# A state space and MLP layer on one core: one block transposed by TensorE, the rest rows of w1 loaded twice, LayerNorm written in one part, and a new order

## The chip, the cores and the metric

The kernel runs on one core of one Trainium2 chip. The core has five engines that run side by side, each with its own list of instructions: TensorE (PE; PEld is its loading of weights), VectorE (DVE), ScalarE (ACT), GpSimd (POOL) and SyncE (SP). SyncE here only issues DMAs, and ScalarE issues a few as well. Engines wait for one another by semaphores. Data are computed on in SBUF, TensorE writes its products into banks of PSUM, and DMAs move data between the chip's memory and SBUF, some of them transposing on the way. The metric is the device time of one execution in microseconds (us); the lower the better.

## The reference

The input x has 2048 tokens of 448 channels. `xn` is its LayerNorm. Two branches read it: a diagonal state space model with 448 complex states, and an MLP with a second LayerNorm, 1792 hidden units, gelu, and silu at its end.

```python
xn = layernorm(x)
# state space branch
dt = exp(log_dt); Lam_bar = exp(dt * Lam)
B_bar = ((Lam_bar - 1) / Lam)[:, None] * B          # B, C complex, 448 x 448
h[t] = Lam_bar * h[t-1] + B_bar @ xn[t]             # 2048 steps
s = 2 * real(C @ h) + xn * Dskip
# MLP branch
g = silu(gelu(layernorm(xn) @ w1 + b1) @ w2 + b2)   # w1 448 x 1792, w2 1792 x 448
out = x + s * g
```

## The kernel before

**Tiles and groups.** The 2048 tokens are worked on in four groups of 512. A group has two blocks of 256 tokens, and a block has two parities: a partition holds two neighbouring tokens, the even one (parity 0) and the odd one (parity 1), so that each tile is 128 tokens of 448 channels. LayerNorm writes two versions of a group: `xn` for the state space branch (buffer `xn_sb`) and `xm` for the MLP, LayerNorm applied twice (buffer `xn2_sb`). The profile's names of buffers don't always tell the two apart on the side of the reader: some rows say `xn_sb` for either. Both are transposed, because TensorE contracts over partitions; the results are `xnT` and `xn2T`.

**The first product, w1.** A channel count of 448 is three blocks of 128 rows and one of 64. All matmuls of `one_mm` (L666) contract over 64 rows, the upper and the lower half of the partitions side by side, so the last 64 rows of w1 are needed on both halves. In the kernel before, chunks of columns of w1 are loaded by SyncE (`ldw1`, L339): chunk 0 of two column blocks of 128, and three of four. One load brings w1's last 64 rows to the upper half of slot 3, and after each chunk a copy by ScalarE or VectorE puts the needed rows on the lower half. For this the LayerNorm rows are laid out as 512 columns that overlap: columns 0 to 383, and then 320 to 447, written as two parts (L410, L451, L452). Products go through gelu on ScalarE (L673) into `gT`.

**Group 0's opening.** `first_stats` (L384) and `first_apply` (L403) make `xm` of group 0 directly. Block 0 is transposed by TensorE, eight transposes against an identity into PSUM (L415), and copied out by VectorE and ScalarE. Block 1 is transposed by a DMA that SyncE issues (L77). `mm1_run` then makes the first product with matmuls 256 wide, block 0 and block 1 mixed. `dummies` (L382) are matmuls of a constant that keep TensorE going before its data are there.

**The rest.** The second product (w2) is L792 and L795 with full rows and the last 64; in the last group L853 makes it with tokens on the partitions. The bias columns of the end, Dskip and b2, are turned by small matmuls (`skip_columns`, L563 and L564) and copied from PSUM into `db`. B_bar is made from the parameters (`parameters`, `tables`, `lb`: L601, L602), and three transposing DMAs make `BT` from `Bn`. The input projection `bu` (L698) multiplies `xnT` by `BT`; VectorE scans (L757); L816, L817, L821 and L822 multiply with C, in the last group L866 and L869. `ln_scale` (L424) makes the factors of LayerNorm out of the statistics, either on VectorE by an inverse root of its own (L431, L432, L436 to L441) or on GpSimd by a power (L431 to L435). A sine for the parameters' complex exponentials is a polynomial on GpSimd (L500 to L506).

**What sets the order.** Nothing is scheduled at run time. Each piece of work is recorded as a task with the names that it reads and writes (`Plan.add`); from these the program works out the semaphore waits. The list `ORDER` says in which order the tasks are given out to the engines' lists, and `SECOND` says which tasks that were recorded with two engines (`either`, L65) take the second one. A DMA is a task of the engine that issues it, and stands in that engine's list: an instruction of SyncE that waits holds up all later DMAs of its queue.

Of the kernel before, what the change touches and what calls it, by code (L numbers as in the profile page):

```python
# [979 lines left out]
```

## Time and profile before

| | |
|---|---|
| median of 3 runs | 144.18 us (144.06 to 144.89) |
| profiled execution | 145.18 us |
| its span | 143.4 us |
| granted TensorE clock | 1.0 |
| PE busy | 137.7 us, 96% of the span |
| DVE busy | 126.0 us, 88% |
| ACT busy | 105.9 us, 74% |
| POOL busy | 24.7 us, 17% |

The profile is of one execution, which took 145.18 us; its span, from the first to the last instruction recorded, is 143.4 us, and all times inside the profile count from the start of that span. A row of a timeline gives the start of a run of equal instructions, how long the run took, the engine, the line of the kernel, the operation with output and inputs, and how many there are; a bracket at the end gives the idle time of the engine just before and what ended it. A matmul's end is modelled, so that two in a row overlap in the rows; where the pace matters, one counts from start to start. A row of grouped instructions has the busy time and the mean of one.

### The profile page before, as it was taken

How to read it: one execution, taken by the hardware profiler on the slowest of the kernel's cores; microseconds unless marked ns; L12 is line 12 of the kernel's file. 1: busy time of each engine (PE TensorE's matmuls, PEld its weight loads, DVE VectorE, ACT ScalarE, POOL GpSimd, SP SyncE). 2: the span in 40 equal slices, each digit the busy share in tenths (PEclk: the TensorE clock that was granted, in tenths of full speed). 3: DMA queues.
4: the chain of work that ended last, by engine and by line, in shares of the span. 5: the costliest groups of instructions: out<-in, count | busy, mean ns of one | idle time of the engine just before them, and what ended most of it. 6: DMA issues, size and time to landing. Idle time of an engine off the chain costs nothing.

```text
span 143.4 us, 3549 instructions
## 1 busy us (share of the span) xinstructions
PE 137.7 (96%) x1422; PEld 90.9 (63%) x1422; DVE 126.0 (88%) x275; ACT 105.9 (74%) x197; POOL 24.7 (17%) x83
## 2 busy tenths in 40 slices
PE   7999998999999989999999999999999999999991
PEld 7879953464455854566558844588777677665560
DVE  2979878998999679999999989993699998999994
ACT  3699959999996879879889359451777999928300
POOL 3389760256000700001000000200000001000000
DMA  4979997799997961010010745099830000003233
GB/s 101 240 238 249 311 331 184 152 245 184 199 189 148 151 134 35 0 32 0 7 32 0 61 108 110 0 199 193 160 126 9 0 5 0 18 5 69 49 119 128
DMA packets 38530, 16.21 MB, mean 113 GB/s; under 512 B 32937, under 2 KB 38066, under 8 KB 38514
## 3 DMA queue, kind: packets, MB, share of 16 engines
q1 hardware_dynamic: 38352, 15.92, 49.5%
q8 instruction: 11, 0.18, 0.5%
q10 hardware_dynamic: 162, 0.07, 0.2%
q14 instruction: 5, 0.04, 0.1%
HBM read 6.09 MB, written 1.84 MB: 55 GB/s over the span
## 4 chain that ended last, share of the span: by engine, by line
PE 63%; DMA 14%; DVE 13%; SPq 4%; ACT 1%; issue 1%; POOL 1%; DVEq 0%; ACTq 0%
PE psum L667 15%; PE psum L698 13%; PE psum L792 9%; PE psum L853 7%; DMA Bn<-in_A_B_re_dram 6%; PE psum L817 5%; DMA xnT<-xn_sb 5%; PE psum L816 5%; PE psum L382 3%; DMA Cr<-in_A_C_im_dram 3%; SPq L78 3%; DVE tmp L601 2%; DVE Bn L602 2%; PE psum L869 2%; PE psum L866 2%; DVE xn_sb L451 2%
## 5 line engine op out<-in xcount | busy, mean ns | idle before, releaser
L667 PE MATMUL psum<-xn2T,w_sb 64*128 64x512 bf16 (+1 forms) x490 | 46.5, 334 | 0.7 <-DMA w_sb<-in_B_w_dram 0.3
L673 ACT ACTIVATE gT<-psum,b1f 128x512 bf16<-128x512 f32 (+1 forms) x70 | 37.5, 607 | 4.5 <-PE psum L667 4.2
L667 PEld LDWEIGHTS psum<-xn2T,w_sb 64*128 64x128 bf16 x490 | 26.6, 108 | 13.9 <-ACT gT L673 1.0
L792 PE MATMUL psum<-gT,w_sb 128*128 128x512 bf16 x126 | 28.0, 379 | 0.7 <-ACT gT L673 0.6
L698 PE MATMUL psum<-xnT,BT 64*128 64x256 bf16 x392 | 25.0, 269 | 0.4 <-DVE u_sb L721 0.4
L698 PEld LDWEIGHTS psum<-xnT,BT 64*128 64x128 bf16 x392 | 19.2, 94 | 6.7 <-issue 1.0
L792 PEld LDWEIGHTS psum<-gT,w_sb 128*128 128x128 bf16 x126 | 11.9, 98 | 15.6 <-issue 1.5
L757 DVE TENSOR_TENSOR_SCAN s_w<-vs,dk 128x1048 f32<-128x1048 bf16 (+1 forms) x8 | 16.3, 2057 | 0.1
L452 ACT ACTIVATE xn_sb<-x_all,lnw 128x448 bf16<-128x448 bf16 (+2 forms) x16 | 10.0, 665 | 5.4 <-DMA xnT<-xn_sb 3.8
L853 PE MATMUL psum<-w_sb,gT 128*128 128x448 bf16 x56 | 10.9, 352 | 0.0
L474 ACT ACT_TABLE_LOAD x8 | 10.3, 1283 | 0.4
L305 ACT ACTIVATE ue<-psum 128x512 bf16<-128x512 f32 (+1 forms) x12 | 6.4, 562 | 5.3 <-PE psum L698 5.2
L451 DVE TENSOR_SCALAR xn_sb<-x_all,lnw 128x448 bf16<-128x448 bf16 (+2 forms) x24 | 8.0, 362 | 0.9 <-DVE lnw L441 0.5
L853 PEld LDWEIGHTS psum<-w_sb,gT 128*128 128x128 bf16 x56 | 5.5, 98 | 4.8 <-ACT psum L305 0.2
L305 ACT ACTIVATE vs<-s_w 64x258 bf16<-64x258 f32 (+2 forms) x11 | 6.5, 612 | 2.7 <-DVE s_w L757 2.6
L816 PE MATMUL psum<-hx,CZ 128*128 128x256 bf16 x63 | 8.4, 275 | 0.0
L817 PE MATMUL psum<-Bn,CQ 128*128 128x256 bf16 x63 | 8.2, 273 | 0.2 <-DVE Bn L777 0.2
L767 POOL TENSOR_TENSOR cur<-ang 128x8 f32<-128x8 f32 x2 | 0.4, 204 | 41.6 <-DVE ang L766 41.6
L798 ACT ACTIVATE g_sb<-psum,db 128x512 bf16<-128x512 f32 (+1 forms) x12 | 7.1, 629 | 0.6 <-PE psum L792 0.6
L369 DVE BATCH_NORM_STATS2 lnst<-x_all 128x6 f32<-128x448 bf16 x12 | 7.1, 613 | 0.4 <-DMA x_all<-in_A_x_dram 0.4
L816 PEld LDWEIGHTS psum<-hx,CZ 128*128 128x128 bf16 x63 | 5.9, 98 | 2.3 <-issue 0.4
L824 DVE TENSOR_TENSOR t<-psum,g_sb 128x512 bf16<-128x512 f32 (+1 forms) x12 | 7.1, 614 | 0.1
(161 smaller groups left out, 207.1 us busy)
## 6 DMA issues: line engine op xcount, KB each, us to landing
x_all<-in_A_x_dram SPq DMA_DIRECT2D x3, 448.0 KB, 4.3
w_sb<-in_B_w_dram SPq DMA_DIRECT2D x3, 448.0 KB, 5.3
out_dram<-Bn SPq DMA_DIRECT2D x6, 224.0 KB, 2.7
w_sb<-in_B_w_dram SPq DMA_DIRECT2D x3, 384.0 KB, 5.5
w_sb<-in_B_w_dram SPq DMA_DIRECT2D x2, 224.0 KB, 4.5
...
```

Source lines behind the costliest of these rows:

```text
L305: kb.either(("act", [lambda e, o=o, i=i: e.activation(o, i, ACT.Copy) for o, i in pairs]), ("dve", [lambda e, o=o, i=i: e.tensor_copy(o, i ...
L451: kb.either(("dve", [lambda e, o=o, i=i: e.tensor_scalar(o, i, rs, nb, op0=ALU.mult, op1=ALU.add) for o, i in parts]), ("act", [lambda e, ...
L452: ("act", [lambda e, o=o, i=i: e.activation(o, i, ACT.Identity, bias=nb, scale=rs) for o, i in parts]),
L474: kb.add("act", lambda e: e.preload_act_table_set(what), reads, writes, sem=name)
L667: return lambda e: e.matmul(dst(bk[k]), w1_sb[rows, d, fcol(2 * j + k)], rhs[rows, d], start=not second and n == 0, stop=second and n == 3)
L673: act(lambda e, k=k, fi=fi: e.activation(gT[:, gb, fi, cols], psum[:, bk[k], cols], ACT.Gelu_apprx_tanh, bias=b1f[:, fi:fi + 1]), ["b1f", ...
L698: fns.append(lambda e, rows=rows, bank=bank, m=m, o=o, n=n: e.matmul(psum[:, bank, c * NK:(c + 1) * NK].rearrange("p (b c) -> p b c", b=2) ...
L757: dve(lambda e, so=so, vi=vi, di=di: e.tensor_tensor_scan(so, vi, di, 0.0, ALU.add, ALU.mult), ["v", "vl", "vz", "dk", "dk01"] + ["v3"] * ...
L792: pe([lambda e, fi=fi: e.matmul(psum[:, bk, :], w2_sb[:, fi, 128 * j:128 * j + 128], gT[:, gb, fi, :], start=fi == 0, stop=fi == NF - 1) f ...
L816: pe([lambda e, k=k: e.matmul(par(psum[:, bk, :], 1), CZ[:, k, cols], halves(hx[:, hb, k, 1:NK + 1]), start=False, stop=k == 6, skip_group ...
L817: pe([lambda e, k=k: e.matmul(par(psum[:, bk, :], 0), CQ[:, k, cols], halves(hz[:, hb, k, :]), start=False, stop=k == 6, skip_group_check= ...
L853: pe([lambda e, fi=fi: e.matmul(P, gT[:, gb, fi, 128 * q:128 * q + 128], w2_sb[:, fi, :], start=False, stop=fi == NF - 1, skip_group_check ...
```

## The change

Five things are changed; all of them end in a new `ORDER` and a new `SECOND`.

1. **Block 1 of group 0.** The transposing DMA of SyncE is gone. `first_apply` now has TensorE transpose block 1 as well: `turn` gives three full transposes and two of 64 columns, one to each half of the partitions, for each parity. Block 0 is done in the same way, so that there are 20 transposes in place of 8, and two more copies out of PSUM, both given to ScalarE. `mm1_run` now starts with more work of block 0 ahead of block 1's.
2. **w1.** Its last 64 rows are loaded twice by ScalarE's queue, to the upper and to the lower half; the copies `w1c_*` are gone. The chunks are three, of 4, 4 and 6 column blocks.
3. **LayerNorm in one part.** `ln_apply` and `first_apply` write 448 columns with one instruction, and a new helper `tail` copies the last 64 of them for the MLP's rows too, so that the transposing DMA finds 512 columns.
4. **Small things.** Dskip's and b2's rows are loaded by SyncE's queue and no longer by ScalarE's; b1 comes in rows of another width, turned by ten small matmuls; one clamp and one negation of the parameters become one instruction and two exponentials; an absolute value may be made by VectorE; four dummies are left out.
5. **Order and engines.** For example, group 1's `ln_scale` was on VectorE and is on GpSimd; group 0's goes the other way. The copy into `db` was ScalarE's and is VectorE's.

Lines move: L667 becomes L660, L698 L691, L792 L785, L795 L788, L415 L375 and L376, L382 L381, L451 L450, L458 L386 (the new helper), L601 and L602 L594 and L595, L305 and L306 L304 and L305.

Three places show the new order. The rows are each engine's instructions as they stand in its list, with the semaphores that they wait for (`s_dve` is VectorE's, `s_d26` that of a DMA).

SyncE's list, before, from the transposition of group 1's `xm` (xn2T) on:

```order
L77 DMA_TRANSPOSE xn2T<-xn_sb 128x16x128 [waits s_dve,s_act]
L78 DMA Bn<-in_A_B_re_dram 64x448
L78 DMA x_all<-in_A_x_dram 128x2x896
L77 DMA_TRANSPOSE xnT<-xn_sb 128x16x128 [waits s_dve]
L77 DMA_TRANSPOSE Cr<-in_A_C_re_dram 128x3x448
L77 DMA_TRANSPOSE Cr<-in_A_C_im_dram 128x3x448
L77 DMA_TRANSPOSE BT<-Bn 128x16x128 [waits s_dve] x2
L77 DMA_TRANSPOSE BT<-Bn 128x24x128 [waits s_dve]
```

The same stretch after the change:

```order
L77 DMA_TRANSPOSE Cr<-in_A_C_re_dram 128x3x448
L77 DMA_TRANSPOSE xn2T<-xn_sb 128x16x128 [waits s_dve]
L77 DMA_TRANSPOSE BT<-Bn 128x16x128
L77 DMA_TRANSPOSE Cr<-in_A_C_im_dram 128x3x448
L77 DMA_TRANSPOSE xnT<-xn_sb 128x16x128 [waits s_dve]
L77 DMA_TRANSPOSE BT<-Bn 128x16x128
L77 DMA_TRANSPOSE BT<-Bn 128x24x128 [waits s_dve]
```

C's first transposition now stands ahead of xn2T's, the first BT right behind it, and group 0's xnT after that; the loads of Bn and x that stood between come ahead of all of these.

TensorE's list, before, around the first matmuls of the input projection (L698), with the second product of group 0 (L792) between:

```order
L698 MATMUL psum<-xnT,BT 128x256 [waits s_d27,s_d26]
L698 MATMUL psum<-xnT,BT 128x256 x11
L792 MATMUL psum<-gT,w_sb 128x512 [waits s_act]
L792 MATMUL psum<-gT,w_sb 128x512 x5
L792 MATMUL psum<-gT,w_sb 128x512 [waits s_act]
L792 MATMUL psum<-gT,w_sb 128x512 x7
L698 MATMUL psum<-xnT,BT 128x256 [waits s_d28]
L698 MATMUL psum<-xnT,BT 128x256 x11
```

And after, where L691 is the input projection and L660 the first product of group 1:

```order
L691 MATMUL psum<-xnT,BT 128x256 [waits s_d25,s_d23,s_d24]
L691 MATMUL psum<-xnT,BT 128x256 x11
L660 MATMUL psum<-xn2T,w_sb 128x512 [waits s_pe]
L660 MATMUL psum<-xn2T,w_sb 128x512 x7
L691 MATMUL psum<-xnT,BT 128x256 [waits s_pe]
L691 MATMUL psum<-xnT,BT 128x256 x15
L660 MATMUL psum<-xn2T,w_sb 128x512 [waits s_act]
L660 MATMUL psum<-xn2T,w_sb 128x512 x5
L691 MATMUL psum<-xnT,BT 128x256 [waits s_act,s_d26]
L691 MATMUL psum<-xnT,BT 128x256 x11
```

The rows that wait for the third BT are those of `s_d28` before and of `s_d26` after. Ahead of them now stand 28 matmuls of the input projection in place of 12, fewer of group 1's first product (90 in place of 98), and none of the 14 of L792, which come later.

VectorE's list, before, where group 1's `xm` is made (L451, ahead of it the last step of `ln_scale`, L441):

```order
L441 SCALAR_TENSOR_TENSOR lnw<-lnmv,lnw 128x8 [waits s_dve]
L451 TENSOR_SCALAR xn_sb<-x_all,lnw 128x384 [waits s_dve,s_d24]
L451 TENSOR_SCALAR xn_sb<-x_all,lnw 128x128
L451 TENSOR_SCALAR xn_sb<-x_all,lnw 128x384
L451 TENSOR_SCALAR xn_sb<-x_all,lnw 128x128
L451 TENSOR_SCALAR xn_sb<-x_all,lnw 128x384 [waits s_dve]
L451 TENSOR_SCALAR xn_sb<-x_all,lnw 128x128
```

And after, from a B_bar step on (L594, L595; L567 are steps of the table `s_w`):

```order
L595 SCALAR_TENSOR_TENSOR Bn<-Bn,cw,tmp 128x512 [waits s_dve]
L567 SCALAR_TENSOR_TENSOR s_w<-dk,cw,s_w 128x258
L305 COPY db<-psum 128x8 [waits s_pe]
L506 TENSOR_TENSOR cw<-cw 128x4
L509 TENSOR_SCALAR cw<-cw 128x4
L595 SCALAR_TENSOR_TENSOR Bn<-Bn,cw,tmp 128x512 [waits s_dve]
L450 TENSOR_SCALAR xn_sb<-x_all,lnw 128x448 [waits s_pool]
L450 TENSOR_SCALAR xn_sb<-x_all,lnw 128x448
L567 SCALAR_TENSOR_TENSOR s_w<-dk,cw,s_w 128x258
L450 TENSOR_SCALAR xn_sb<-x_all,lnw 128x448 [waits s_dve] x2
L567 SCALAR_TENSOR_TENSOR s_w<-dk,cw,s_w 128x258
L386 COPY xn_sb<-xn_sb 128x4x64 [waits s_dve]
```

The copy into `db` is now here, and `xm` waits for GpSimd's `ln_scale` (`s_pool`), is made in four instructions, and has the tail copy behind it.

The diff, with the numbers of `ORDER` and `SECOND` cut to a line each and the comparisons of small indices left out:

```diff
-14 363 16 41 0 9 10 15 1 17 13 2 11 3 22 12 5 18 4 19 21 90 23 26 24 91 93 42 25 89 28 92 94 30 43 95 104 103 45 44 64 109 105 50 46 96 20 110 47 108
+14 0 16 36 9 10 2 11 5 15 17 3 13 1 12 19 18 4 23 24 84 20 25 21 85 37 87 22 83 35 38 86 88 40 8 39 89 27 41 105 44 97 28 42 45 102 7 106 98 43 57 90
...
-29 31 45 51 53 54 60 61 62 63 64 65 78 79 80 82 83 84 111 181 204 205 206 208 210 212 216 218 220 229 234 236 238 242 250 254 256 258 270 274 278 328
+41 44 47 48 49 51 55 56 60 62 64 67 72 76 78 79 82 101 170 171 172 173 177 201 204 206 208 212 214 216 225 228 230 232 234 236 238 242 244 250 273 277
...
-            CH = ((0, 2), (2, 4), (6, 4), (10, 4))
+            CH = ((0, 4), (4, 4), (8, 6))
...
                 ld("sp", w1_sb[:, 0:3, a:a + w], dram_ap(B_w1, a, [[F, 128], [128 * F, 3], [1, w]]), [f"w1_{c}"])
-                copy([(w1_sb[0:64, 3, a:a + w], w1_sb[64:128, 2, a:a + w])], [f"w1_{c}"], [f"w1c_{c}"])
...
+            for h in (1, 0):
+                ld("act", w1_sb[64 * h:64 * h + 64, 3, :], dram_ap(B_w1, 384 * F, [[F, 64], [1, F]]), [f"w1r{h}"])
             ldw1(0)
-            ld("sp", w1_sb[64:128, 3, :], dram_ap(B_w1, 384 * F, [[F, 64], [1, F]]), ["w1r"])
...
-            def tcols(b, par, d):
-                a = par * 512 + (0, 128, 256, 320)[d]
-                return xn2_sb[:, b, a:a + 128]
+            def turn(b, par, bank):
+                row, o = xn2_sb[:, b, par * 512:par * 512 + D], psh[:, bank, 0:512].rearrange("p (d c) -> p d c", d=4)
+                return [lambda e, d=d: e.transpose(o[:, d], row[:, 128 * d:128 * d + 128], ident[:, :]) for d in range(3)] \
+                    + [lambda e, h=h: e.transpose(o[h, 3], row[:, 384:D], ident[:, :]) for h in (slice(0, 64), slice(64, 128))]
...
+            def tail(rows, keys):
+                v = rows.rearrange("p b (r c) -> p (b r) c", r=2)
+                o, i = v[:, :, D:512], v[:, :, 384:D]
+                kb.either(("dve", lambda e: e.tensor_copy(o, i)), ("act", lambda e: e.activation(o, i, ACT.Copy)), keys, keys)
...
-                    if b:
-                        continue
                     bank, oap = 6 - par, xn2T[:, 0, b, par * 4:par * 4 + 4, :]
-                    pe([lambda e, d=d, par=par, bank=bank: e.transpose(psh[:, bank, d * 128:(d + 1) * 128], tcols(b, par, d), ident[:, :]) for d in range(4)],
+                    pe(turn(b, par, bank),
                        [f"xm{b}p{par}", "ident", f"xm{b}"], [f"ps{bank}"])
...
-                if b:
-                    kb.dma("sp", xn2T[:, 0, 1, :, :], xn2_sb[:, 1, :], reads=["xm1p0", "xm1p1", "xm1"], writes=["xmT1p0", "xmT1p1"], transpose=True)
...
-                parts = [(row[:, 0:384], src[:, 0:384]), (row[:, 384:512], src[:, 320:D])] if which else [(row[:, 0:D], src)]
...
+                row = row[:, 0:D]
+                kb.either(("dve", lambda e: e.tensor_scalar(row, src, rs, nb, op0=ALU.mult, op1=ALU.add)),
+                          ("act", lambda e: e.activation(row, src, ACT.Identity, bias=nb, scale=rs)),
...
+                tail(src[:], [("xn", "xm")[which] + str(b) for b in range(2)])
...
-                    rows, d = slice(64 * h, 64 * h + 64), (0, 1, 2 + h, 3 - h)[n]
+                    rows, d = slice(64 * h, 64 * h + 64), n
...
-                   xk2 + [f"w1_{c}", "w1r"] + ([f"w1c_{c}"] if second else []), [f"ps{bk[0]}", f"ps{bk[1]}"], split=True)
+                   xk2 + [f"w1_{c}"] + ["w1r0", "w1r1"] * second, [f"ps{bk[0]}", f"ps{bk[1]}"], split=True)
...
-            dummies(4, ["st0"])
...
-            mm1_run(0, ((0, 0), (1, 1), (2, 2), (3, 3), (4, 0), (5, 1), (6, 2)))
+            mm1_run(0, ((0, 0), (1, 1), (2, 2), (3, 0), (4, 1), (5, 2), (6, 0)))
...
-            mm1_run(1, ((0, 3), (1, 0), (2, 1), (3, 2), (4, 0), (5, 1), (6, 2)))
+            mm1_run(1, ((0, 1), (1, 3), (2, 2), (3, 0), (4, 1), (5, 3), (6, 2)))
```

More of the change, by code (lines that the diff above doesn't have):

```diff
@@ L228, in bass_recurrent_scan__ssm_conv_s5__mixer_channel_mlp__prompt_kernel @@
         vrows = dk.bitcast(BF)[:, 1, 0:512]
-        brows = vrows[32:36, :]
+        brows = dk.bitcast(BF).rearrange("p i c -> p (i c)")[32:35, 2 * NS:2 * NS + 768]
         cw = SB("cw", [128, 32, 4], F32)
@@ L449, in ln_apply @@
                 src = x_all[:, 2 * g + b, par, :]
-                parts = [(row[:, 0:384], src[:, 0:384]), (row[:, 384:512], src[:, 320:D])] if which else [(row[:, 0:D], src)]
-                kb.either(("dve", [lambda e, o=o, i=i: e.tensor_scalar(o, i, rs, nb, op0=ALU.mult, op1=ALU.add) for o, i in parts]),
-                          ("act", [lambda e, o=o, i=i: e.activation(o, i, ACT.Identity, bias=nb, scale=rs) for o, i in parts]),
+                row = row[:, 0:D]
+                kb.either(("dve", lambda e: e.tensor_scalar(row, src, rs, nb, op0=ALU.mult, op1=ALU.add)),
+                          ("act", lambda e: e.activation(row, src, ACT.Identity, bias=nb, scale=rs)),
                           [f"lnw{g % 2}_{b}"] + xk(2 * g + b), [key])
-            def tail_twice():
-                v = xn_sb[:].rearrange("p b (r c) -> p (b r) c", r=2)
-                o, i = v[:, :, D:512], v[:, :, 384:D]
-                kb.either(("dve", lambda e: e.tensor_copy(o, i)), ("act", lambda e: e.activation(o, i, ACT.Copy)), ["xn0", "xn1"], ["xn0", "xn1"])
             def ln(g, which):
@@ L463, in ln @@
                         ln_apply(g, b, par, which)
-                if not which:
-                    tail_twice()
                 src, dst = (xn_sb, xn2_sb)[which], (xnT, xn2T)[which]
+                tail(src[:], [("xn", "xm")[which] + str(b) for b in range(2)])
                 key, kT = ("xn", "xm")[which], ("xnT", "xmT")[which] + str(g % 2)
@@ L490, in parameters @@
                 small(lambda e: e.tensor_tensor(col(A1), col(DT), col(LRE), ALU.mult), ["cdt", "cp"], ["ca"])
-                small(lambda e: e.tensor_scalar(col(A1), col(A1), -DECAY_MAX, None, op0=ALU.max), ["ca"], ["ca"])
-                small(lambda e: e.tensor_scalar(col(NA1), col(A1), -1.0, None, op0=ALU.mult), ["ca"], ["cna"])
-                act(lambda e: e.activation(cw[:, R1:RI + 1, :], cw[:, A1:NA1 + 1, :], ACT.Exp), ["ca", "cna"], ["cr"])
+                small(lambda e: e.tensor_scalar(col(NA1), col(A1), -DECAY_MAX, -1.0, op0=ALU.max, op1=ALU.mult), ["ca"], ["cna"])
+                act([lambda e: e.activation(col(R1), col(NA1), ACT.Exp, scale=-1.0), lambda e: e.activation(col(RI), col(NA1), ACT.Exp)], ["cna"], ["cr"])
                 small(lambda e: e.tensor_tensor(ang[:, 0, 0, 0, :], col(DT), col(F2), ALU.mult), ["cdt", "f2"], ["f1"])
@@ L508, in parameters @@
                 small(wrap, ["f1", "f3", "f4"], ["f1"], True)
-                act(lambda e: e.activation(YB, YA, ACT.Abs), ["f1", "f2"], ["f1"])
+                kb.either(("act", lambda e: e.activation(YB, YA, ACT.Abs)), ("dve", lambda e: e.scalar_tensor_tensor(out=YB, in0=YA, scalar=-1.0, in1=YA, op0=ALU.mult, op1=ALU.max)),
+                          ["f1", "f2"], ["f1"])
                 small(sine, ["f1"], ["as", "ac"], True)
@@ L556, in b1_columns @@
             def b1_columns():
-                pe([lambda e, k=k: e.matmul(psum[:, 4, 2 + k:11 + k:4], brows[0:4, k:512:4], ident[32:36, 32:35], start=True, stop=True) for k in range(4)]
-                   + [lambda e, k=k: e.matmul(psum[:, 4, k:k + 1], brows[0:4, k:256:2], ident[32:36, 35:36], start=True, stop=True) for k in range(2)],
+                pe([lambda e, k=k: e.matmul(psum[:, 4, k:5 + k:4], brows[:, k:512:4], ident[32:35, 32:34], start=True, stop=True) for k in range(4)]
+                   + [lambda e, k=k: e.matmul(psum[:, 4, 8 + k:9 + k], brows[:, k:768:6], ident[32:35, 34:35], start=True, stop=True) for k in range(6)],
                    ["br", "br0", "br1", "ident"], ["ps4"])
@@ L853, in mm2_tokens @@
                 pe([lambda e, fi=fi: e.matmul(P, gT[:, gb, fi, 128 * q:128 * q + 128], w2_sb[:, fi, :], start=False, stop=fi == NF - 1, skip_group_check=True)
-                    for fi in range(NF)], [f"gT{gb}_{fi}_{h}" for fi in range(NF) for h in range(2)] + [f"w2_{c}" for c in range(4)], [f"ps{bk}"])
+                    for fi in range(NF)], [f"gT{gb}_{fi}_{h}" for fi in range(NF) for h in range(2)] + [f"w2_{c}" for c in range(len(CH))], [f"ps{bk}"])
                 act(lambda e: e.activation(g3[:, q, :], P, ACT.Silu), [f"ps{bk}", f"Ws{g}"], [f"g3_{q}"])
```

18 lines of the change are left out of this document (8 added, 10 removed), and 35 rows, old and new, of the table ORDER.

## The prediction

> **What bounds the kernel now.** I read the page's busy shares first, then TensorE's waits, TensorE's own timeline, and sums by stretch.
>
> ```profile
> span 143.4 us, 3549 instructions
> PE 137.7 (96%) x1422; PEld 90.9 (63%) x1422; DVE 126.0 (88%) x275; ACT 105.9 (74%) x197; POOL 24.7 (17%) x83
> ```
>
> TensorE is busy in 96% of the span, so a faster neighbour gains only what TensorE waits. Its recorded waits (reader, releaser, us, times, longest):
>
> ```profile
> PE psum L792 <- ACT gT L673: 0.6, 1, 0.6
> PE psum L698 <- DVE u_sb L721: 0.4, 1, 0.4
> PE psum L667 <- DMA w_sb<-in_B_w_dram: 0.3, 1, 0.3
> PE psum L667 <- ACT gT L673: 0.2, 1, 0.2
> PE psum L817 <- DVE Bn L777: 0.2, 1, 0.2
> ```
>
> These five add to 1.7 us: 0.3 ahead of the first matrix product, 0.8 behind ScalarE's gelu, 0.6 behind VectorE. The timeline places them (start, duration, line; idle before in brackets), and also shows where work merely runs:
>
> ```profile
> 23.20 5.77 PE L792 MATMUL psum<-gT,w_sb 128*128 128x512 bf16 x26 [0.59 <-ACT gT L673]
> 41.57 0.82 PE L698 MATMUL psum<-xnT,BT 64*128 64x256 bf16 x12
> 42.52 3.19 PE L792 MATMUL psum<-gT,w_sb 128*128 128x512 bf16 x14
> 45.65 2.58 PE L698 MATMUL psum<-xnT,BT 64*128 64x256 bf16 x44
> 48.16 1.72 PE L795 MATMUL psum<-gT,w_sb 128*64 128x256 bf16 x28
> 49.81 0.83 PE L698 MATMUL psum<-xnT,BT 64*128 64x256 bf16 x12
> 51.00 1.26 PE L698 MATMUL psum<-xnT,BT 64*128 64x256 bf16 x20 [0.36 <-DVE u_sb L721]
> 91.25 0.96 PE L816 MATMUL psum<-hx,CZ 128*128 128x256 bf16 x7
> 92.38 0.94 PE L817 MATMUL psum<-Bn,CQ 128*128 128x256 bf16 x7 [0.17 <-DVE Bn L777]
> 93.15 0.95 PE L816 MATMUL psum<-hx,CZ 128*128 128x256 bf16 x7
> ```
>
> And by stretch (window, its length, TensorE busy and count, weight loads, DVE, ACT, POOL, granted clock, DMA share, GB/s):
>
> ```profile
> 7.36:18.71 11.35, 11.21 (x196) 10.21 (x197) 10.00 (x41) 11.02 (x28) 9.53 (x30) 1.00 0.89 270
> 18.98:30.55 11.57, 10.98 (x72) 5.39 (x71) 10.21 (x40) 9.71 (x17) 3.48 (x15) 1.00 0.88 224
> 30.55:41.57 11.02, 10.82 (x100) 5.26 (x100) 10.52 (x25) 10.58 (x17) 3.35 (x5) 1.00 1.07 188
> 45.65:140.44 94.79, 94.26 (x962) 62.30 (x961) 85.90 (x145) 66.83 (x120) 5.17 (x12) 1.00 0.31 62
> ```
>
> In the last stretch, two thirds of the span, TensorE lacks only 0.5 us of being busy throughout. So the change is decided before 45.65. There DMA runs at 0.88 to 1.07 of its engines, and the chain of transposing DMAs that makes BT ends just ahead of its reader:
>
> ```profile
> 22.45 2.91 SPq L77 DMA_TRANSPOSE xn2T<-xn_sb  x1
> 26.72 3.25 SPq L77 DMA_TRANSPOSE xnT<-xn_sb  x1
> 33.70 5.17 SPq L77 DMA_TRANSPOSE BT<-Bn  x2
> 39.83 3.69 SPq L77 DMA_TRANSPOSE BT<-Bn  x1
> BT<-Bn SPq DMA_TRANSPOSE x1, 5.5
> ```
>
> The last row is the third BT's time from issue to landing: 39.83 + 5.5 = 45.3, and its matmuls begin at 45.65. That margin of 0.3 us is no wait today; it is the next thing that can be late.
>
> **Term 1, start of the first product.** The first w1 chunk grows from 256 to 512 columns, and w1's last rows now travel on ScalarE's queue beside it. Loads of the opening took, from issue (KB each, us):
>
> ```profile
> w_sb<-in_B_w_dram SPq DMA_DIRECT2D x3, 384.0 KB, 5.5
> w_sb<-in_B_w_dram SPq DMA_DIRECT2D x1, 192.0 KB, 3.6
> ```
>
> TensorE waited 0.3 for the small chunk; a 384 KB one took 1.9 more, but with four other loads ahead of it. I bound the shift at 0 to 0.9 and take 0, since term 2's wait absorbs a late start. The Trainium skill, "DMA: Bandwidth & Descriptors", section "Issuing engines are not separate DMA queues", says that transfers issued by different engines run on the same 16 DMA engines and interleave, so a second queue saves issue time only. By it the upper bound of 0.9 is the likelier end; no row of before has two large loads on two queues.
>
> **Term 2, block 1's transposes on TensorE.** Ten transposes at the price of the eight that are there: 0.62 us for eight on the path,
>
> ```profile
> 5.57 0.62 PE psum L415 x8
> L415 PE MATMUL psum<-ident,xn_sb x8: 219/246/314, 5.4 to 6.0; 128*128 128x128 bf16 x8
> ```
>
> so 10 x 0.62/8 = **0.78 us**, not hidden, since TensorE is what is late. Each one's own duration (the second row: 219 to 314 ns, median 246) is three times its share of the chain: they run overlapped, and the step of 0.078 counts. The Trainium skill, "TensorE: Matmul & The Clock Gate", section "Part 4: PE-mode transpose", gives about 275 ns for one 128x128 bf16 transpose in a kernel; by that ten would cost 2.75, an estimate. The trace has that as a duration, not as a step.
>
> The transposes stand behind 42 of the 196 matmuls, so TensorE arrives at 7.36 + 42 x 0.0579 (11.35/196) = 9.8. They read xm of block 1:
>
> ```profile
> 8.85 0.60 DVE L410 TENSOR_SCALAR xn_sb<-x_all,lnmv,lnw 128x384 bf16<-128x384 bf16 x2 [0.47 <-POOL lnw L397]
> ```
>
> That is finished at 9.45 before. The new order puts some seven more VectorE instructions ahead of it, two of them wide (s_w steps); I estimate 10.4. The two PSUM copies of block 1 follow on ScalarE, while 154 matmuls behind them wait. I take a wait of **0.6**, bounds 0 to 1.2. Against it: ScalarE loses its two w1 copies, which stood between TensorE and its gelus, so the stage's idle time of 11.35 - 11.21 = 0.14 may go, and its matmuls may take the pace of those at 45.65, (48.16 - 45.65)/44 = 0.057 instead of 0.0579, which is 196 x 0.0009 = 0.18. I take both back, 0.3 (bounds 0 to 0.6). Sum for the stage: 0.78 + 0.6 - 0.3 = **+1.1**.
>
> **Term 3, gelu and the bias column.** The last two gelus of the stage stood behind LayerNorm work on ScalarE (two instructions of L452), and a matmul of the second product waited for them. That work is gone from there, so the 0.59 wait at 23.20 goes: **-0.6**. What is late next is the copy of the bias columns `db` out of PSUM, which moves from ScalarE to VectorE:
>
> ```profile
> 19.55 0.18 ACT L305 ACTIVATE db<-psum 128x8 f32<-128x8 f32 x1
> ```
>
> Before, it ran right behind the gelus, at 19.55, while TensorE used other banks. On VectorE it now stands behind four LayerNorm statistics, B_bar work and four s_w steps, and TensorE's ninth matmul of the second product waits for it, because it writes to that PSUM bank; the whole second product is queued behind. TensorE comes there at 18.71 + 1.1 for the first product, 0.3 for the bias columns and 8 x 10.98/72 = 1.2, which is 21.3. VectorE's work ahead of it was in part done at 24 to 27 before, behind work that has now moved away; I estimate 22.3, no row showing that order: **+1.0**, bounds 0 to 2.
>
> **Term 4, TensorE's arrival at the third BT.** Against 45.65 of before: +1.1 - 0.6 + 1.0; the 0.2 wait on gelu in the 30.55 stretch goes (-0.2); eight matmuls of the first product come later (8 x 10.82/100 = -0.87); sixteen of the input projection come earlier (16 x 0.057 = +0.91); the fourteen of the second product that stood at 42.52 come later (45.65 - 42.52 = -3.13). Arrival 45.65 + 1.1 - 0.6 + 1.0 - 0.2 - 0.87 + 0.91 - 3.13 = **43.9**. Work left over for afterwards: 3.13 + 0.87 - 0.91 = 3.1.
>
> **Term 5, the third BT itself.** LayerNorm's scale of group 1 moves from VectorE to GpSimd, behind the sine, small coefficient work and a copy of Bn.
>
> ```profile
> 9.70 0.19 POOL L431 TENSOR_SCALAR lnw<-lnmv 128x4 f32<-128x4 f32 x1
> 12.95 0.48 POOL L435 TENSOR_SCALAR lnw<-lnw 128x8 f32<-128x8 f32 x1
> 13.39 0.39 POOL L500 TENSOR_SCALAR ang<-ang 128x16 f32<-128x16 f32 x1
> 16.64 0.22 POOL L506 TENSOR_TENSOR ang<-ang 128x16 f32<-128x16 f32 x1
> L513 POOL TENSOR_TENSOR cw<-cw 128x4 f32<-128x4 f32 x10 | 1.9, 204 | 2.6 <-DVE cw L513 2.5
> L612 POOL COPY Bn<-Bn 128x64 bf16<-128x64 bf16 x1 | 0.7, 690 | 4.5 <-DMA Bn<-in_A_B_re_dram 4.5
> 20.60 1.76 DVE L451 TENSOR_SCALAR xn_sb<-x_all,lnw 128x384 bf16<-128x384 bf16 x6 [0.53 <-DVE lnw L441]
> 12.84 1.28 DVE L574 SCALAR_TENSOR_TENSOR s_w<-dk,cw,s_w 128x258 f32<-128x258 f32 x3
> ```
>
> A scale on GpSimd takes 12.95 + 0.48 - 9.70 = 3.7. The sine takes 16.64 + 0.22 - 13.39 = 3.5 and can start about when the scale of before did, 9.8. Then 18 small instructions at 0.2 (3.6), the copy of Bn at 0.7 to 2 for six times as many columns (1.2), waits for VectorE of about 1.5 (2.5 before), and the scale: 9.8 + 3.5 + 3.6 + 1.2 + 1.5 + 3.7 = 23.3. VectorE then needs four applications and the tail copy, 5 x 0.29 (1.76/6), and two s_w steps at 0.43 (1.28/3): 23.3 + 1.5 + 0.9 = **25.7** for the transposition that started at 22.45 before. From there SP issues xn2T, BT, C, xnT, BT, BT; before, from 26.72, xnT, C, C, BT, BT, BT: as many of much the same sizes, 45.3 - 26.72 = 18.6 to the last landing, of which 39.83 - (33.70 + 5.17) = 0.96 was a wait of the third BT, half of which I keep. So 25.7 + 18.1 = **43.8**. It comes level with TensorE's 43.9, so I take no wait; the price past that point is one to one.
>
> **Terms hidden.** LayerNorm in one part shortens VectorE's and ScalarE's work, with a tail copy added; either is hidden where TensorE is dense, as are the skip vectors on SP, which are read late. b1's ten small matmuls instead of six lie ahead of TensorE's start, whose cover is the wait of term 2; uncovered they cost 4 x 0.078 = 0.3. The four dummies removed stand before that too.
>
> **The rest.** Two later waits go, taken from start to start: 51.00 - 49.81 - 12 x 0.057 = 0.51, and (92.38 - 91.25) - (93.15 - 92.38) = 0.36. I put 0.2 back for one new wait of the smallest size above: **-0.65** (bounds -0.9 to 0). End, as the last products are unchanged.
>
> **Sum.** 43.9 - 45.65 + 3.1 - 0.65 = +0.7. The profiled execution took 145.18 (span 143.4, 1.8 around it) and lies 1.0 above the median of 144.18. So 145.9 for such an execution, **144.9** as a median.
>
> **Rivals.**
> *(a) The transposes become the bound: slower.* DMA is saturated (1.07) while they run. If the issues ahead of the third BT are all long (2.91 for xn2T, 3.25 for xnT, and 5.17/2 = 2.6 for each of two BT; C within the same 2.6), the third BT is issued at 25.7 + 2.91 + 3.25 + 3 x 2.6 + 0.96 = 40.6 and lands 5.5 later, at 46.1. TensorE then waits 46.1 - 43.9 = 2.2 for it: 144.9 + 2.2 = 147.1. It decides from 43.9 on. For it: the margin was 0.3. Against: the loads that competed until 30 are issued earlier now. Chance 0.16.
> *(b) No new wait.* GpSimd and VectorE are in time for TensorE everywhere: -0.59 - 0.2 - 0.87 + 0.78 = -0.9, median 143.3; with 0.3 to 0.6 of pace regained, 143.0 to 142.7. For it: every one of the three waits I added is under 1.2 us and estimated from rows of another order. Chance 0.28, and 0.13 of it, where an end is a little earlier still, over 1% faster.
> *(c) The transposes don't overlap.* Standing alone between waits, each would cost its own duration: 10 x 0.246 = 2.46 in place of 0.78, +1.7, and 146.6. Against: the eight of before, in two groups of four behind two waits, did overlap. Chance 0.03. The skill's 275 ns, used as a step, is this case.
> *(d) VectorE is late,* for `db` (2.0) and xm (1.2) both: +1.6, 146.5. Chance 0.09.
>
> **Numbers.** The forecast has 0.44. Its own range: 0.6 either way for xm, 1.0 for `db`, which partly cover each other: 143.9 to 145.9. One per cent, 1.4 us, is about what measurement of this kernel tells from no change: 142.7 to 145.6. Of the forecast's 0.44, 0.38 lies within it and 0.06 above; of (b) 0.13 below, 0.15 within; (a), (c), (d) lie above, 0.28. Faster 0.13, same 0.53, slower 0.34. Range 142.9 to 146.9: it leaves out the lower part of (b), about 0.1, and half of (a), 0.08.
>
> **What would show it.** Right: ten more transposes in 0.7 to 0.9 us; a wait on VectorE's xm of block 1 near 10; no wait on gelu near 23, one on `db` at the ninth matmul of the second product; group 1's xn2T transposition issued near 25.7; third BT landing within 0.5 us of its reader. Wrong: TensorE dense between 10 and 45 (b); third BT landing past 45 with TensorE idle (a).

## The result: 4.4% slower, and the profile after

The changed kernel takes 150.6 us (median of 4 runs, 149.87 to 151.69) beside 144.32 of the kernel before; the ratio is 1.0436, with a 95% interval of 1.0356 to 1.0515. The profiled execution took 149.87, with a span of 148.1 us against 143.4: 4.7 us to be explained.

TensorE's waits in the profile after, in the columns used before:

```profile
PE psum L660 <- ACT g_sb L791: 1.5, 1, 1.5
PE psum L660 <- issue: 1.5, 1, 1.5
PE psum L691 <- DMA BT<-Bn: 0.4, 1, 0.4
```

The waits for gelu and for VectorE are gone. Two new ones of 1.5 us stand in their place, both longer than any wait of before. Its timeline up to the third BT, and the place of the later wait:

```profile
6.95 1.03 PE L381 MATMUL psum<-const-bfloat16-1.0 128*128 128x128 bf16 x8
7.95 1.47 PE L660 MATMUL psum<-xn2T,w_sb 64*128 64x256 bf16 x12
10.87 2.08 PE L660 MATMUL psum<-xn2T,w_sb 64*128 64x256 bf16 x30 [1.45 <-issue]
12.88 0.34 PE L375 MATMUL psum<-ident,xn_sb 128*128 128x128 bf16 x3
...
13.79 8.60 PE L660 MATMUL psum<-xn2T,w_sb 64*128 64x256 bf16 x154
22.32 1.04 PE L785 MATMUL psum<-gT,w_sb 128*128 128x512 bf16 x4
...
33.52 8.45 PE L660 MATMUL psum<-xn2T,w_sb 64*128 64x512 bf16 x76
...
45.36 2.60 PE L691 MATMUL psum<-xnT,BT 64*128 64x256 bf16 x40 [0.35 <-DMA BT<-Bn]
...
64.35 0.84 PE L660 MATMUL psum<-xn2T,w_sb 64*128 64x512 bf16 x6 [1.47 <-ACT g_sb L791]
```

From these rows and those of before:

| up to | before | after | difference |
|---|---|---|---|
| end of group 0's first product | 18.71 | 22.32 | +3.6 |
| end of its second product | 30.55 | 33.52 | +3.0 |
| the third BT's reader, 3.1 us of other work put off | 45.65 | 45.36 | +2.8 |
| end of TensorE's last matmul | 140.44 | 144.44 | +4.0 |
| end of the span | 143.4 | 148.1 | +4.7 |

The first stage makes most of the loss: of its 3.6 us, 0.6 are a later start (7.95 against 7.36), 2.5 lie in the first 42 matmuls, 0.9 are the ten transposes, and the other 154 matmuls gave 0.4 back. TensorE takes from 7.95 to 12.88 for 42 matmuls, 4.9 us where the pace of before gives 2.4. It stops after 12 of them. The name "issue" in the bracket says only that the profile shows no engine that it waited for. In the list of instructions the thirteenth matmul waits for the two loads of w1's last rows. How long these took, from issue to landing (median us, two of 224 KB):

```profile
w_sb<-in_B_w_dram ACTq DMA_DIRECT2D x2, 224.0 KB, 7.3
```

ScalarE issued them at 2.52 and 3.12; they landed at 9.51 and 10.78, and TensorE went on at 10.87. In the kernel before, the one load of such rows took 4.6.

On VectorE the copy of `db` now waits for TensorE, and the transposition of group 1's `xm` starts late, as SyncE's queue shows:

```profile
23.67 0.17 DVE L305 COPY db<-psum 128x8 f32<-128x8 f32 x1 [2.72 <-PE psum L557]
26.83 2.62 SPq L77 DMA_TRANSPOSE xn2T<-xn_sb  x1
36.80 6.20 SPq L77 DMA_TRANSPOSE BT<-Bn  x2
```

The second product's ninth matmul didn't wait for `db`. The third BT landed at 45.31 and TensorE waited 0.35 for it.

From there to its last matmul TensorE idles 1.54 us (99.08 less 97.54 busy) where it idled 0.53 before, mostly in the wait for `g_sb`, the silu that ScalarE makes of the second product:

```profile
45.36:144.44 99.08, 97.54 (x967) 63.13 (x967) 86.29 (x150) 70.52 (x126) 10.35 (x9) 1.00 0.30 64
```

The end, before and then after:

```profile
139.61 0.83 PE L869 MATMUL psum<-CQ,Bn 128*128 128x224 bf16 x7
139.74 1.79 SPq L78 DMA_DIRECT2D out_dram<-w_sb  x4
140.79 0.57 DVE L872 TENSOR_TENSOR w_sb<-w_sb,x_all 128x448 bf16<-128x448 bf16 x2
```

```profile
142.60 0.33 SPq L78 DMA_DIRECT2D out_dram<-Bn  x1
142.94 1.50 PE L862 MATMUL psum<-CQ,Bn 128*128 128x224 bf16 x14
144.67 1.79 SPq L78 DMA_DIRECT2D out_dram<-w_sb  x4
144.79 0.45 DVE L865 TENSOR_TENSOR w_sb<-w_sb,x_all 128x224 bf16<-128x224 bf16 x2
```

Behind TensorE's last matmul the span goes on for 3.7 us (148.1 - 144.44), 0.7 more than before (143.4 - 140.44 = 3.0). VectorE is over as soon behind TensorE as it was (144.79 + 0.45 against 140.79 + 0.57). It is SyncE that is late: it begins its last four output DMAs 0.2 us behind TensorE's end, where it began them 0.7 ahead of it. The program has SyncE wait, ahead of its last four DMAs, until the others have landed (L118), and one of the others, an output of group 2, is issued only at 142.60.

So the 4.7 us are 2.8 at the third BT's reader, 1.0 of further idle time of TensorE, 0.7 of tail, and 0.2 in which TensorE is busy longer.

### The profile page after: what moved, and what is told of

Its sections match the earlier page's. It is cut to its first block, busy times and chain, and to the rows that moved or that the text cites. A ratio compares the mean times of both kernels' runs of the same rounds, so it can differ in the third digit from the quotient of the medians.

```text
span 148.1 us, 3557 instructions
## 1 busy us (share of the span) xinstructions
PE 140.2 (95%) x1434; PEld 92.4 (62%) x1434; DVE 122.9 (83%) x272; ACT 105.4 (71%) x194; POOL 29.3 (20%) x76
## 4 chain that ended last, share of the span: by engine, by line
PE 62%; DVE 12%; DMA 11%; POOL 5%; SPq 3%; issue 2%; ACT 1%; ACTq 1%; DVEq 0%
PE psum L660 21%; PE psum L691 11%; PE psum L846 7%; PE psum L785 7%; PE psum L809 5%; DMA w_sb<-in_B_w_dram 5%; PE psum L810 5%; DMA Cr<-in_A_C_im_dram 3%; SPq L77 3%; DMA x_all<-in_A_x_dram 3%; DVE CZ L595 2%; DVE tmp L594 2%; DVE lnst L367 2%; PE psum L859 2%; PE psum L814 2%
## 5 line engine op out<-in xcount | busy, mean ns | idle before, releaser
L660 PE MATMUL psum<-xn2T,w_sb 64*128 64x512 bf16 (+1 forms) x490 | 47.4, 338 | 3.0 <-ACT g_sb L791 1.5
L660 PEld LDWEIGHTS psum<-xn2T,w_sb 64*128 64x128 bf16 x490 | 27.5, 116 | 16.3 <-issue 2.6
L785 PE MATMUL psum<-gT,w_sb 128*128 128x512 bf16 x126 | 27.9, 379 | 0.0
L691 PE MATMUL psum<-xnT,BT 64*128 64x256 bf16 x392 | 24.9, 269 | 0.4 <-DMA BT<-Bn 0.4
L691 PEld LDWEIGHTS psum<-xnT,BT 64*128 64x128 bf16 x392 | 18.7, 94 | 7.0 <-DMA BT<-Bn 0.8
L785 PEld LDWEIGHTS psum<-gT,w_sb 128*128 128x128 bf16 x126 | 12.0, 98 | 14.5 <-issue 0.6
L762 POOL CAST vs<-cur 128x8 bf16<-128x8 f32 x2 | 1.8, 890 | 52.7 <-DVE cur L760 52.7
L304 ACT ACTIVATE vs<-s_w 64x258 bf16<-64x258 f32 (+2 forms) x11 | 6.7, 612 | 5.7 <-DVE s_w L750 5.6
L304 ACT ACTIVATE ue<-psum 128x512 bf16<-128x512 f32 (+1 forms) x12 | 6.1, 546 | 6.0 <-PE psum L691 6.0
L450 DVE TENSOR_SCALAR xn_sb<-x_all,lnw 128x448 bf16<-128x448 bf16 x20 | 7.4, 387 | 0.0
L451 ACT ACTIVATE xn_sb<-x_all,lnw 128x448 bf16<-128x448 bf16 x8 | 6.0, 757 | 1.7 <-POOL lnw L434 1.7
```

The lines of the kernel that those rows point to most:

```text
L304: kb.either(("act", [lambda e, o=o, i=i: e.activation(o, i, ACT.Copy) for o, i in pairs]), ("dve", [lambda e, o=o, i=i: e.tensor_copy(o, i ...
L450: kb.either(("dve", lambda e: e.tensor_scalar(row, src, rs, nb, op0=ALU.mult, op1=ALU.add)), ("act", lambda e: e.activation(row, src, ACT. ...
L660: return lambda e: e.matmul(dst(bk[k]), w1_sb[rows, d, fcol(2 * j + k)], rhs[rows, d], start=not second and n == 0, stop=second and n == 3)
L691: fns.append(lambda e, rows=rows, bank=bank, m=m, o=o, n=n: e.matmul(psum[:, bank, c * NK:(c + 1) * NK].rearrange("p (b c) -> p b c", b=2) ...
L785: pe([lambda e, fi=fi: e.matmul(psum[:, bk, :], w2_sb[:, fi, 128 * j:128 * j + 128], gT[:, gb, fi, :], start=fi == 0, stop=fi == NF - 1) f ...
```

## The experiments

The theory 'rows' said that the loads of w1's last rows are the main loss, 'pace' that TensorE ran at half pace in the opening. For the pace, compare the eight dummies at 6.95 above (1.03 us) with the same eight in the kernel before:

```profile
6.38 0.64 PE L382 MATMUL psum<-const-bfloat16-1.0 128*128 128x128 bf16 x8
```

All comparisons below are with the kernel before, run beside on the same chip (145.1 us for the runs e1 to e4, 145.3 for e5 to e8, 144.6 for e9 to e11), so ratios are compared, not times.

### w1's rows on SyncE's queue

```diff
-                ld("act", w1_sb[64 * h:64 * h + 64, 3, :], dram_ap(B_w1, 384 * F, ...
+                ld("sp", w1_sb[64 * h:64 * h + 64, 3, :], dram_ap(B_w1, 384 * F, ...
 # in ORDER: behind w1_0, ahead of w1_1
```

> The changed kernel, with the two loads of w1's last rows issued by SyncE between the first and the second w1 chunk, not by ScalarE. In the changed kernel they land at 9.51 and 10.78, and TensorE stops until 10.87. Theory 'rows' (that stop is the main loss): in a queue of their own turn they land near 8.5, the stop shrinks from 1.45 us to under 0.3, and the time falls by 1.3 to 2.5 us from 150.6, to 148 to 149. Theory 'pace' (TensorE runs at half pace up to 10.87, 0.21 us a pair of matmuls instead of 0.11, and this is the loss): the stop goes, but the half pace lasts on into the later matmuls and eats up half or more of it; 149.5 to 150.5.

Run e1: 148.33 us, ratio 1.0193 (1.0105 to 1.0281). The loads took 5.0 us (7.3). Issued at 2.66 and 3.26, some 0.14 us later than in the change, they landed at 7.46 and 8.54, 2 us earlier, and the stop is gone:

```profile
7.92 3.32 PE L660 MATMUL psum<-xn2T,w_sb 64*128 64x256 bf16 x42
20.60 1.04 PE L785 MATMUL psum<-gT,w_sb 128*128 128x512 bf16 x4
43.68 2.60 PE L691 MATMUL psum<-xnT,BT 64*128 64x256 bf16 x40 [0.34 <-DMA BT<-Bn]
62.95 0.84 PE L660 MATMUL psum<-xn2T,w_sb 64*128 64x512 bf16 x6 [1.34 <-ACT g_sb L791]
```

It falls out as 'rows' said: by the two ratios, 2.4 of the 4.4% are this one choice of queue, with the place in it. The rows didn't gain at the cost of other loads. The second and third chunk of w1, issued 1.2 and 1.3 us later here, landed at 9.39 and 10.97, against 11.36 and 12.93 in the change; from 8 to 11 the DMA engines were as busy in both (shares of 1.07 and 1.05), but moved 367 GB/s here and 276 there. Why two queues moved less wasn't tried.

What is left of the loss in this run's profile (span 146.7, 3.3 longer than before) is 1.1 us at the third BT's reader, the first product still ending 1.9 later than before; 1.5 us more up to TensorE's last matmul; and 0.7 in the tail.

### The dummies back, alone and with the rows

```diff
+            dummies(4, ["st0"])
             first_apply(0)
             b1_columns()
 # in ORDER: these ahead of block 0's transposes, b1's matmuls behind them
```

> The changed kernel, with the four dummy matmuls ahead of block 0's transposes back, and the small matmuls of b1 behind these transposes, as in the kernel before. Theory 'rows': the first matmuls start some 0.6 us earlier, at full pace, and then wait for the rows until 10.8 all the same; the time stays within 0.5 us of 150.6. Theory 'pace': the pace doubles near 5.8, as before, and the time falls by 0.8 to 1.5 us, to 149 to 149.8. In both, a pair of matmuls is 0.11 us apart at 8 if the dummies are what sets the pace, and 0.21 if they are not.

Run e2: 152.32 us, ratio 1.0469 (1.0392 to 1.0545), no better than the change itself. The opening runs at full pace, and TensorE then stops longer, and after the stop falls to half pace. The timeline, and the sums of two stretches (after PE busy and count come the other engines; the granted clock is the third figure from the end):

```profile
7.45 0.84 PE L660 MATMUL psum<-xn2T,w_sb 64*128 64x256 bf16 x12
10.33 2.74 PE L660 MATMUL psum<-xn2T,w_sb 64*128 64x256 bf16 x30 [2.04 <-issue]
...
14.37 10.42 PE L660 MATMUL psum<-xn2T,w_sb 64*128 64x256 bf16 x154
```

```profile
14.37:18.00 3.63, 3.63 (x38) 2.56 (x38) 3.52 (x14) 1.14 (x3) 3.07 (x14) 0.50 1.03 360
18.50:24.60 6.10, 6.10 (x116) 5.99 (x112) 2.09 (x5) 5.79 (x16) 2.72 (x5) 1.00 0.69 101
```

So with the dummies the first twelve matmuls take 0.84 in place of 1.47, as 'pace' said, but the time gains nothing, since TensorE then waits for the rows until 10.33. The fall to half pace wasn't expected; the first product ends 2.4 us later than in the change, at 24.72. That the dummies alone set the pace of the opening isn't shown either: two runs further down, e6 and e7, leave them out too, and their profiles have the opening at full pace.

> Both edits of the two kernels above. Both theories: the gains add up or more, since the stop no longer hides the pace; first product over at 19.6 to 20.3 in place of 22.32, time 147 to 148.3. If neither is what costs, it stays at 150.

Run e3: 149.35 us, ratio 1.0245 (1.0152 to 1.0338): no better than the rows alone, against both theories. TensorE started at 7.45 at full pace and then stopped for 0.74 until 9.04, since here the rows landed at 8.95. The first product ended at 20.66 (20.60 with the rows alone). What the pace would save, the rows take back.

### One load of rows in the kernel before

```diff
-                copy([(w1_sb[0:64, 3, a:a + w], w1_sb[64:128, 2, a:a + w])], [f"w1_{c}"], [f"w1c_{c}"])
+            ld("act", w1_sb[0:64, 3, :], dram_ap(B_w1, 320 * F, [[F, 64], [1, F]]), ["w1c"])
```

> The kernel before, with one part of the change alone: the lower half's rows of w1 come by a load of ScalarE's queue (64 x 1792, as many bytes as one of the two of the change) and no longer by four copies on ScalarE and VectorE. Theory 'rows': the load shares the DMA engines with the first chunk and the other rows and lands at 9 or later, TensorE's second half of the first pair of column blocks, at 8.0 before, waits 1 us or more; 145 to 146.5. Rival (a load is as good as the copies): the time stays at 144.3 or falls by up to 0.3.

Run e4: 145.82 us beside 145.09, ratio 1.0040 (1.0007 to 1.0073). The place was another one than expected. This load landed at 7.76, in time; but the one on SyncE's queue beside it landed at 7.96 (7.32 before), and the first product started late and then fell to half pace:

```profile
8.04 12.87 PE L666 MATMUL psum<-xn2T,w_sb 64*128 64x256 bf16 x196 [1.19 <-DMA w_sb<-in_B_w_dram]
```

```profile
8.81:12.02 3.21, 3.21 (x34) 2.84 (x32) 3.11 (x14) 1.03 (x3) 2.81 (x7) 0.50 0.94 165
```

The first product ended 2.1 us later (20.85), the third BT's reader came 1.1 later (46.75), the span grew by 0.7. The kernel before takes up two thirds of a delay in its first stage in waits that it has anyway.

### db on ScalarE, and g_sb ahead of LayerNorm

Both start from the rows on SyncE's queue.

```diff
 # SECOND: without the copy of db (ScalarE again, ahead of silu's table)
```

> The changed kernel with w1's last rows on SyncE's queue (as in the run of that name, 148.33 us), and the copy of db on ScalarE in place of VectorE, ahead of silu's table. In that run VectorE stood before the copy until TensorE had made the bias columns, and group 1's transposition was issued at 25.10 and the third BT landed at 43.63, with TensorE waiting 0.34 for it. Theory 'db holds the chain': the transposition is issued 1 us or more earlier, the third BT lands before 43, the 0.34 wait goes; the time falls by 0.3 to 0.5 us. Rival (the chain is set by GpSimd's LayerNorm scale): issue stays within 0.4 us of 25.1, no gain.

Run e5: 148.4 us, ratio 1.0213 (1.0167 to 1.0259). The transposition was issued at 24.51 (25.10), the third BT landed at 43.31 and the wait for it is gone. It was less than the 1 us or more forecast, because GpSimd's LayerNorm scale, over at 22.1, comes next. No gain is measured: TensorE waits 1.5 for g_sb and 0.6 for the next xn2T (1.3 and 0.4 with the rows alone).

```diff
 # ORDER: ScalarE's L451 of group 3 behind the last g_sb of group 1, not ahead
```

> The changed kernel with w1's last rows on SyncE's queue, and on ScalarE the last g_sb of group 1 ahead of the LayerNorm application that waits for GpSimd's scale of group 3 (it stood behind it; TensorE waited 1.3 us for that g_sb). Theory 'queued behind the scale': TensorE's 1.3 us wait goes entirely and the time falls by 1.0 to 1.3 us, to about 147.1. Rival (the LayerNorm of group 3 is needed as early as that itself): the wait moves to another place within some us, and the time falls by less than 0.4.

Run e6: 148.33 us, ratio 1.0182 (1.0117 to 1.0247): no gain against 1.0193. The g_sb wait went, and a wait of 0.88 for gelu came at the same place:

```profile
65.33 0.84 PE L660 MATMUL psum<-xn2T,w_sb 64*128 64x512 bf16 x6 [0.88 <-ACT gT L666]
```

The rival comes nearer here: ScalarE is behind in this stretch, and which of its instructions TensorE waits for is second to that. (The profiled execution, 145.2 us of span, had its opening at full pace without the dummies: the nine dummies at 4.00, ahead of b1's matmuls, took 0.75 in place of 1.14, and the first product started at 7.33. The edit changes nothing there, so its times are not put down to the edit.)

Why ScalarE is behind is seen on GpSimd, which it waits for. Group 3's LayerNorm scale in the changed kernel took 61.51 + 1.64 - 55.85 = 7.3 us, while its twin of group 1 took 3.2:

```profile
55.85 0.81 POOL L430 TENSOR_SCALAR lnw<-lnmv 128x4 f32<-128x4 f32 x1 [19.88 <-DVE lnmv L371]
59.67 1.75 POOL L433 TENSOR_TENSOR lnw<-lnmv,lnw 128x8 f32<-128x8 f32 x1
61.51 1.64 POOL L434 TENSOR_SCALAR lnw<-lnw 128x8 f32<-128x8 f32 x1
```

```profile
18.44 0.26 POOL L430 TENSOR_SCALAR lnw<-lnmv 128x4 f32<-128x4 f32 x1 [0.63 <-DVE lnmv L371]
21.11 0.21 POOL L433 TENSOR_TENSOR lnw<-lnmv,lnw 128x8 f32<-128x8 f32 x1
21.40 0.25 POOL L434 TENSOR_SCALAR lnw<-lnw 128x8 f32<-128x8 f32 x1
```

In the kernel before this scale started at 46.47 and took 3.2. The new order loads group 3's x at 45.66 (26.05 before), and so the scale falls beside VectorE's work for the scan. That this work is what slows it wasn't tried.

### Block 1 by DMA again

```diff
+                    if b:
+                        continue
 ...
+                if b:
+                    tail(xn2_sb[:, 1:2, :], ["xm1p0", "xm1p1"])
+                    kb.dma("sp", xn2T[:, 0, 1, :, :], xn2_sb[:, 1, :], ..., transpose=True)
```

> The changed kernel with w1's last rows on SyncE's queue, and block 1 of group 0 transposed by a DMA again (with a tail copy on VectorE), no transposes of block 1 on TensorE and no copies of them on ScalarE. Theory 'ten transposes cost their spacing': the stretch of 0.9 us (11.17 to 12.07) goes from TensorE; if the DMA lands ahead of its reader the time falls by 0.6 to 0.9 us. Rival (the DMA lands late or holds loads up behind it on SyncE's queue): TensorE waits for it or for what is behind it, and the time is the same or longer.

Run e7: 156.29 us, ratio 1.0753 (1.0713 to 1.0792). The rival holds, by far more than it said. The DMA took 9.2 us from issue to landing, against 3.2 before, and TensorE waited for it:

```profile
19.61 8.95 PE L665 MATMUL psum<-xn2T,w_sb 64*128 64x256 bf16 x120 [6.36 <-DMA xn2T<-xn_sb]
```

In the new order loads of Bn, x and w2 are issued ahead of it, and the last of these landed at 17.96, the transposition itself at 19.57 (381 GB/s moved from 10.2 to 14). That it waited for their bytes is the likely reason; no run takes them away. Beside that the ten transposes on TensorE, 0.9 us, are cheap in this order.

### All suspects mended together

```diff
-            for h in (1, 0):
-                ld("act", w1_sb[64 * h:64 * h + 64, 3, :], ...
+            ld("sp", w1_sb[64:128, 3, :], ..., ["w1r1"])
+                copy([(w1_sb[0:64, 3, a:a + w], w1_sb[64:128, 3, a:a + w])], ["w1r1"], [f"w1q_{c}"])
+            dummies(4, ["st0"])
 # db on ScalarE; L451 of group 3 behind the last g_sb of group 1
```

> The changed kernel with all suspected causes taken away together: w1's last rows loaded once on SyncE's queue and copied to the lower half by VectorE in three chunks; the four dummies back and b1's small matmuls behind block 0's transposes; db on ScalarE; the last g_sb of group 1 ahead of the LayerNorm application. If these are the causes, TensorE has no stop above 0.5 us ahead of 60, and the first product is over by 19.5; the end is within 0.7 us of the kernel before, 144.4 to 145.8. If something else costs too, it stays above 146.5.

Run e8: 149.0 us, ratio 1.0264 (1.0224 to 1.0304). It falls out against the expectation. The opening has stops of 0.5 and 0.2 only, but the first product is over at 20.4 (20.6 in e1), not by 19.5, and the third BT isn't there:

```profile
45.96 2.60 PE L694 MATMUL psum<-xnT,BT 64*128 64x256 bf16 x40 [1.72 <-DMA BT<-Bn]
```

TensorE waited 2.7 us in all for BT. GpSimd's scale was over at 23.2 (21.65 in the changed kernel), the transposition was issued at 25.61, and from there to the third landing it took 20.3 us, not 18.5. TensorE came to the first BT at 40.06, 1.75 us earlier than in the changed kernel, and the third BT landed at 45.9, 0.6 later: the prediction's rival (a) at work. In e1 TensorE came as early (40.12) and waited only 0.34 for the third BT, so it is the transposes that this run made late; which of its edits did that isn't shown. So the causes don't add up.

### The opening, and gelu, in the kernel before

```diff
-            dummies(4, ["st0"])
 # ORDER: b1's matmuls and their copy ahead of block 0's transposes
```

> The kernel before, with one part of the change's opening alone: the four dummy matmuls ahead of block 0's transposes left out, and b1's small matmuls (six here) ahead of these transposes, not behind. w1's rows are as before, in time. Theory 'pace' (small matmuls in place of dummies keep TensorE at half pace): transposes 0.11 us apart, the first product's pairs 0.21 apart up to about 9, its start within 0.5 us of 7.36; the first product ends 0.6 to 1.2 us later than 18.71, and the time rises by 0.3 to 1.0 us. Rival (the pace doesn't depend on these): no change, within 0.2 us.

Run e9: 144.79 us beside 144.64, ratio 0.9999 (0.9961 to 1.0037). The half pace is there, 0.82 for the eight dummies, 1.18 for the first 14 matmuls, and the first product ends at 19.39, 0.7 later. At the third BT's reader (45.60) nothing is left of it. The pace alone costs this kernel nothing.

```diff
 # ORDER: the last two gelus of group 0 ahead of ScalarE's L452 of group 1
```

> The kernel before, with the last two gelus of group 0 ahead of the two LayerNorm instructions on ScalarE, where they stood behind. ScalarE was idle for 1.52 us ahead of these, so that the gelus fit there. The step 'the 0.59 wait on gelu goes' alone: TensorE's wait at 23.20 goes, the third BT still lands near 45.3, now on the path, with a wait of 0.2 to 0.4 for it; the time falls by 0.2 to 0.6 us. Rival (the third BT takes it all back): no change.

Run e10: 144.66 us beside 144.64, ratio 0.9988 (0.9955 to 1.0022), no measurable change. The profiled execution took 146.28 us, with its first product 2.5 us late (from 18.71 to 21.20), and says little about the edit: the wait at the second product is gone in it, and one of 0.35 for gelu stands at 44.21. The 0.59 us of before were not 0.59 us of the time.

### The tail

```diff
 # e6, with db on ScalarE; ORDER: group 2's last L834 and its output DMA
 # ahead of the L864 of group 3 that they stood behind
```

> The changed kernel with w1's last rows on SyncE's queue, the last g_sb of group 1 ahead of the LayerNorm application, db on ScalarE, and one instruction of group 2's output on VectorE (L834, with its output DMA) ahead of the two of group 3 that it stood behind. Theory 'the tail waits for that DMA': from TensorE's end to the end of the span 2.7 us or less, as before (143.4 - 140.44 = 3.0), against 3.7 in the changed kernel; the time lies 0.5 to 0.7 us below the run with the g_sb moved alone (148.3), at 147.6 to 147.8. Rival (the tail's length has another cause): 3.5 us or more still.

Run e11: 147.25 us, ratio 1.0159 (1.0089 to 1.0229), 0.3 us better than e6 by the ratios, well inside both intervals. From TensorE's end (142.28) to the end of the span (145.4) it takes 3.1 us, against 3.7 in the changed kernel and in e6, and 3.0 before. That is not the 2.7 or less of the theory, and far from the rival's 3.5: in the profile nearly all of the longer tail was SyncE's wait for that output DMA. The gain in time, 0.3 of the 0.5 to 0.7 us forecast, is not clear of the noise.

No version here beats the kernel before.

## Why the prediction was wrong, step by step

By parts, forecast and measured: +1.3 and +2.8 us at the third BT's reader, -0.65 and +1.2 from there to TensorE's last matmul, 0 and +0.7 behind it.

**Term 1, the start of the first product, failed.** It took 0 of a bound of 0 to 0.9, and looked only at the first matmul and the first chunk. The first twelve matmuls were late by 0.6 (7.95); the thirteenth needs both loads of the last rows, whose landing was never priced. The row of the one such load before gave 4.6 us, and two of them beside 384 KB chunks took 7.3. TensorE waited 1.45 for them, until 10.87, and moving them to the other queue gave back 2.4% (e1, the difference of two ratios with intervals of 0.8 to 0.9% either way). The bound of 0.9 was too small: the first product ended 3.6 us later, where +1.1 was forecast for the stage. The rule of the Trainium skill quoted there ("DMA: Bandwidth & Descriptors", "Issuing engines are not separate DMA queues"), that transfers issued by different engines interleave, fits rows that land late. That loads issued beside and behind them (chunks of w1, x at 14.14 against 12.17) landed 2 us later than in e1 as well goes beyond it.

**What was put under "terms hidden" was hidden by something else than was said.** The four dummies and b1's matmuls were said to cost 0.3 if uncovered, by their own length. In the profile of the change TensorE's step was nearly twice as long until the stop (1.47 us for twelve matmuls at 7.95, against 0.84 in e2), a cost that the prediction didn't have. It was covered, though not by term 2's wait but by the rows (e2, e3), and in the kernel before it is covered too (e9). That it follows from the missing dummies is not sure: e6 and e7 lack them as well and show full pace.

**Term 2 held in size.** The ten transposes took 13.79 - 12.88 = 0.91 against 0.78. The wait of 0.6 for xm didn't come: xm was ready at 9.84 and TensorE at 12.88. The faster pace came, behind the transposes: 0.4, where 0.3 was taken. The rival of transposes that don't overlap is out.

**Term 3 held for gelu in the profile, and failed for db in its direction.** The second product took 11.20 in place of 11.84, so 0.64 came back. VectorE was at the copy at 20.95, not 22.3; TensorE came to the bias columns at 23.3, and VectorE waited 2.72 for it. What was queued behind that wait was not the second product but group 1's `xm`, and with it all transposes.

**Terms 4 and 5 came out close to each other by luck.** Both sides were late, each for a reason that the prediction didn't have. TensorE's arrival was 45.0 (43.9 forecast), the third BT 45.31 (43.8). From the first of the six issues to the third BT's landing it took 18.5 us (18.1). GpSimd's scale was over at 21.65, earlier than the 23.3 forecast; but VectorE was held at `db` until 23.67, and so the issue came at 26.83 against 25.7.

**"The rest" and the end failed.** The two later waits of before went, 0.87 as worked out. But the new one was 1.47, not 0.2: ScalarE behind GpSimd's stretched scale. And "as the last products are unchanged" overlooked what stands behind them: 0.7 us of longer tail.

**The rivals.** All of them priced TensorE against the transposes or VectorE; none had the rows. So the range ended at 146.9. (a) decided in e8, where TensorE was earlier and the transposes were later.
